# The gate product of the sixth attention unit on VectorE: one step moved between engines in a fused attention and two-layer expert kernel

## The chip, the core and the metric

The program runs on one core of one Trainium2 chip. The metric is the device time of one execution in microseconds (us); the time before is the median of three runs. The engines are named as in the profile: PE is TensorE's matmul stream and PEld its weight loads, DVE is VectorE, ACT is ScalarE, POOL is GpSimd, SP is SyncE, which issues the DMAs.

## What is computed

The reference is a gated linear attention (an mLSTM) over 2 batches, 8 heads, 768 positions and head size 40, followed by two dense layers over the 1536 tokens:

```
m_new = max(f + m, i);  C = exp(f+m-m_new)*C + exp(i-m_new)*outer(v, k)
n = exp(f+m-m_new)*n + exp(i-m_new)*k
y = sigmoid(o) * (C q) / max(|n.q|, 1)                    # per position
h = max(x@w1, x@w2, x@w3);  z = h @ w_out                 # 320 -> 768 -> 320
g = mish(z @ w_in);         out = g @ w_out2              # 320 -> 2048 -> 320
```

The change touches one product in the third line: the output gate sigmoid(o) times the reciprocal of the denominator.

## The kernel before, in words

The attention is cut into 12 units: 6 chunks of 128 positions by 2 batches, unit u being chunk u//2 of batch u%2. The sixth unit is u = 5. Within a unit everything has 128 positions on the partitions. `attend(u)` loads the unit, spreads the decay factors over a PSUM bank with 8 matmuls (`spread`, L141), scans them on DVE (`decay`, L126), forms the scores q.k on PE (`scores`, L164, 16 matmuls as the trace counts them) into the same two banks, multiplies the two on DVE (`decayed`, L169), scales values and keys on POOL (`values` L175, `keys` L186), and takes the sigmoid of the output gate on ACT into the tile `sg` (`gateo`, L190). `passed` (L152) and `queries` (L180) bring in the state of the chunk before.

`finish(u)` ends a unit. `numer` (L206, L208) forms numerator and denominator in one PSUM bank, tile `it`. `denom` takes the denominator: two small DVE steps (L214, L215), a reciprocal on DVE (L216), then the product sg = sg * den over 128 x 320 elements on the engine it is given (L218), GpSimd unless told otherwise. `gated` multiplies `it` by `sg` on DVE into the tile `xn` (L223) and lets ACT copy the last 64 columns once more as padding (L224). `transpose_x` turns `xn` into three 128 x 128 blocks on PE (L235): the first two blocks read what DVE wrote, the third one also reads what ACT copied. ACT then copies the result to `xh` (L237), and `lower_x` (L248, L249) forms the low part on ACT and POOL. `outer` (L258, 6 matmuls in the trace) and `carry` (L270, L272) update the state.

Beside the attention the first dense layer runs: `up(blk, m)` is three groups of eight matmuls (L345), each into a bank of its own; ACT copies the first bank out (L360), DVE takes the maximum with the other two (L362), ACT rounds (L364), POOL forms the low part (L365). In the stretch of the change these matmuls are what PE does between the attention's steps. The weights come as packed 64-bit numbers: ACT rescales both halves (`scaled`, L291 and L292), DVE merges them (`merge`, L299 and L301), and `split_lhs` splits the result into a high part on ACT (L312 to L314) and a low part on POOL (L315 to L317). The unpacked tile `dec` has two buffers, so L291 of a weight waits until POOL's L317 of the weight two before has read its buffer.

Units 0 to 3 are ordered by hand; there the fourth unit's product is already on VectorE. From unit 4 on, the order on each engine is made by a planner. The program is written as a list of steps,

```
PLAN0 = "w2 a4 w3 u0.1 a5 w4 b4 w5 w6 b5 a6 w7 w8 a7 u0.2 b6 u0.3 u0.4"
```

(`a` attend, `b` finish, `w` load a weight of the first layer, `u` up), followed by PLAN1 with three loads of the second weight (`o0 o1 o2`), more units and the `down` matmuls (L376 to L384). The planner goes through a timeline of its own estimated costs; whenever an engine is free there, it gets the earliest step of the list that is ready at that moment. Then the order is fixed, and on the chip each engine works through its own list in that order, each instruction waiting for its semaphores. Where an estimate and the chip differ, an instruction can wait at the head of its engine while others behind it could run. PE's order in the second dense layer (L659) is again written by hand.

Of the kernel before, what the change touches and what calls it, by code (L numbers as in the profile page):

```python
# [44 lines left out]
def mlstm_moe_kernel(ctx, tc, fi0, fir, qk2, q3, nat, w13, wo1, wi2, wo2, ident, bmask, out):  # L45
    nc = tc.nc
# [150 lines left out]
    def numer(u, ps=None):  # L197
        c, b = u // B, u % B
        t = unit[u]
        ps = itbank(f"it{u}") if ps is None else ps  # L200
        it = heads(ps[:, 0:H * VD], VD)
        vt = vps[u % 2]
        for g in range(3):
            h1 = min(3 * g + 3, H)
            if c > 0:
                nc.tensor.matmul(it[:, 3 * g:h1], t["cb"][:, g], st[b][:, 3 * g:h1], start=True, stop=False)  # L206
            for h in range(3 * g, h1):
                nc.tensor.matmul(it[:, h], t["dt"][:, h], vt[:, h], start=(c == 0), stop=(c == 0 or h == h1 - 1))  # L208
        t["it"] = it

    def denom(u, eng=nc.gpsimd):
        num = unit[u]["it"]
        den = a2.tile([P, H, 1], F32, tag="den", name=f"den{u}")
        nc.vector.tensor_scalar(den, num[:, :, D:VD], -1.0, 1.0, op0=ALU.mult, op1=ALU.max)  # L214
        nc.vector.tensor_tensor(den, den, num[:, :, D:VD], op=ALU.max)  # L215
        nc.vector.reciprocal(den, den)  # L216
        sg = unit[u]["sg"]
        eng.tensor_tensor(sg, sg, den.to_broadcast([P, H, D]), op=ALU.mult)  # L218

    def gated(u):  # L220
        t = unit[u]
        xn = a2.tile([P, 3 * P], F32, tag="xn", name=f"xn{u}")
        nc.vector.tensor_tensor(heads(xn[:, 0:DM], D), t["it"][:, :, 0:D], t["sg"], op=ALU.mult)  # L223
        nc.scalar.activation(xn[:, DM:3 * P], xn[:, 2 * P:DM], AF.Copy)  # L224
        t["xn"] = xn

    def transpose_x(u, xp=None, fill=0):
        xh, xl = xs[u // 4]
        col = u % 4 * L
        xn = unit[u]["xn"]  # L230
        xp = bank("sm", f"xp{u}") if xp is None else xp
        dummy(xp, fill)
        xp = xp[:, 0:3 * L].rearrange("p (j t) -> p j t", j=3)
        for j in range(3):
            unit[u]["pe"] = nc.tensor.transpose(xp[:, j], xn[:, j * P:(j + 1) * P], idt[:, 0:P])  # L235
        unit[u]["xp"] = xp
        return nc.scalar.activation(xh[:, :, col:col + L], xp, AF.Copy)  # L237

    def lower_x(u):
        xh, xl = xs[u // 4]  # L240
        col = u % 4 * L
        if u < B:
            xr = m1.tile([P, 3, L], F32, tag=f"hl{4 + u}", bufs=1, name=f"xr{u}")
            nc.scalar.activation(xr, unit[u]["xp"], AF.Copy)
            return lambda: nc.gpsimd.tensor_tensor(xl[:, :, col:col + L], xr, xh[:, :, col:col + L].bitcast(F32), op=ALU.subtract)
        if u >= 4:
            xr = a2.tile([P, 3, L], F32, tag="xr", bufs=1, name=f"xr{u}")
            nc.scalar.activation(xr, unit[u]["xp"], AF.Copy)  # L248
            return nc.gpsimd.tensor_tensor(xl[:, :, col:col + L], xr, xh[:, :, col:col + L].bitcast(F32), op=ALU.subtract)  # L249
        return nc.vector.tensor_tensor(xl[:, :, col:col + L], unit[u]["xp"], xh[:, :, col:col + L].bitcast(F32), op=ALU.subtract)  # L250

    def outer(u, sp=None, fill=0):
        sp = bank("sm", f"sp{u}") if sp is None else sp
        dummy(sp, fill)
        sp = sp[0:120, 0:9 * VD].rearrange("p (h e) -> p h e", h=9)
        kt, vt = kps[u % 2], vps[u % 2]
        for g in range(3):
            pe = nc.tensor.matmul(sp[:, 3 * g:3 * g + 3], kt[:, 3 * g:3 * g + 3].rearrange("p h e -> p (h e)"), vt[:, 3 * g:3 * g + 3], start=True, stop=True)  # L258
        unit[u]["sp"] = sp
        return pe  # L260

    def carry(u):
        c, b = u // B, u % B
        sp = unit[u]["sp"]
        if c == 0:
            return nc.vector.tensor_tensor(st[b], sp[:, 0:H], bmt[:, 0:H].unsqueeze(2).to_broadcast([120, H, VD]), op=ALU.mult)
        dc = unit[u]["dc"]
        for g in range(3):
            h1 = min(3 * g + 3, H)
            nc.scalar.activation(st[b][:, 3 * g:h1], st[b][:, 3 * g:h1], AF.Copy, scale=dc[:, g])  # L270
        for j in range(3):
            nc.vector.scalar_tensor_tensor(st[b][:, j::3], sp[:, j:H:3], bmt[:, j:j + 1], st[b][:, j::3], op0=ALU.mult, op1=ALU.add)  # L272
# [296 lines left out]

    def finish(u):  # L570
        numer(u)
        denom(u)
        gated(u)
        transpose_x(u)
        lower_x(u)
        if u < NU - B:
            outer(u)
            carry(u)

    act = dict(u=up, d=down, w=load_w13, o=load_wo, a=attend, b=finish)  # L580

    def follow(plan):
# [279 lines left out]
```

## Time and profile before

| what | us |
|---|---|
| median of three runs | 396.18 (396.0 to 398.92) |
| the profiled execution, whole | 398.92 |
| its span, first to last instruction | 397.1 |
| PE busy | 384.9 (97% of the span) |
| DVE busy | 192.3 (48%) |
| ACT busy | 186.9 (47%) |
| POOL busy | 150.0 (38%) |

The profile shows the profiled execution, so what is read from it is a difference within 397.1 us. Busy shares are averages over three stages: attention with the first layer's upper half, the rest of the first layer, and the second layer, where only PE is busy nearly all the time. The mean granted clock of TensorE over the span is 0.987 of full speed.

### The profile page before, as it was taken

What the parts mean: (1) busy time and instruction counts of PE and PEld (TensorE: products, weight loads), DVE (VectorE), ACT (ScalarE), POOL (GpSimd) and SP (SyncE); (2) the same over time, 40 slices, a digit from 0 to 9 for tenths busy, and PEclk for the clock granted to TensorE, in tenths of its full rate; (3) what the DMA queues carried; (4) which work ended last, traced back from release to release, by engine and by line L of the source; (5) the groups of instructions that cost most, each with busy time, mean ns of one, the idle gap of its engine ahead of it and who ended that gap; (6) DMA issues with size and microseconds to landing.
All of it is one profiled execution on the core that took longest, in us unless ns stands there. A gap on an engine that the chain in (4) does not pass through costs nothing.

```text
span 397.1 us, 7598 instructions
## 1 busy us (share of the span) xinstructions
PE 384.9 (97%) x3098; PEld 335.2 (84%) x3098; DVE 192.3 (48%) x297; ACT 186.9 (47%) x382; POOL 150.0 (38%) x151
## 2 busy tenths in 40 slices
PE   8999899899999999999999999998999999999996
PEld 4788788688988888888788789887989899999986
DVE  6899988579454294208621165657222131311212
ACT  3548877726433233165721386886242242423222
POOL 6666897845623133357831036565000020000000
PEclk9899999969999999999999999999999999999999
DMA  7697573634430030003500034500010000100001
GB/s 195 206 281 245 185 247 114 207 120 158 143 104 1 2 132 2 0 2 81 179 5 0 0 134 143 193 2 0 15 55 2 2 2 2 66 2 2 2 2 66
DMA packets 10415, 32.70 MB, mean 82 GB/s; under 512 B 1405, under 2 KB 4285, under 8 KB 10381
## 3 DMA queue, kind: packets, MB, share of 16 engines
q1 hardware_dynamic: 10381, 32.23, 25.0%
q8 instruction: 24, 0.39, 0.4%
q14 instruction: 10, 0.08, 0.1%
HBM read 30.26 MB, written 1.97 MB: 81 GB/s over the span
## 4 chain that ended last, share of the span: by engine, by line
PE 65%; DVE 11%; ACT 11%; POOL 5%; issue 4%; DMA 3%; POOLq 0%; DVEq 0%; ACTq 0%; SPq 0%
PE o L659 16%; PE h L659 15%; PE mm L345 15%; PE it L208 4%; DMA raw_w<-in_w_dram 2%; PE sc L164 2%; PE mz L376 2%; PE mz L377 2%; PE mz L378 2%; ACT g L687 2%; DVE dec_wo L299 2%; DVE dt L126 1%; ACT gh L686 1%; PE fp L141 1%; PE it L206 1%
## 5 line engine op out<-in xcount | busy, mean ns | idle before, releaser
L659 PE MATMUL h<-zh,wi 64*128 64x512 f32 x480 | 88.9, 392 | 2.4 <-ACT g L687 2.2
L659 PE MATMUL o<-wo,gh 64*128 64x320 f32 (+1 forms) x736 | 90.0, 306 | 0.0
L659 PEld LDWEIGHTS o<-wo,gh 64*128 64x128 f32 (+1 forms) x736 | 85.5, 185 | 1.5 <-issue 0.4
L688 DVE TENSOR_TENSOR gl<-g,gh 128x512 fp32r<-128x512 f32 x48 | 37.4, 785 | 98.7 <-ACT g L687 98.5
L659 PE MATMUL o<-wo,gl 64*128 64x320 f32 (+1 forms) x368 | 84.6, 306 | 0.0
L659 PEld LDWEIGHTS h<-zh,wi 64*128 64x128 f32 x480 | 66.9, 185 | 12.7 <-ACT g L687 4.5
L345 PE MATMUL mm<-xh,w 128*128 128x512 f32 x270 | 73.7, 400 | 1.9 <-DVE st L272 1.2
L659 PE MATMUL h<-zl,wi 64*128 64x512 f32 x240 | 70.2, 390 | 0.0
L659 PEld LDWEIGHTS o<-wo,gl 64*128 64x128 f32 (+1 forms) x368 | 68.0, 185 | 0.0
L686 ACT ACTIVATE gh<-h 128x512 fp32r<-128x512 f32 x48 | 28.9, 602 | 75.9 <-PE h L659 75.9
L345 PEld LDWEIGHTS mm<-xh,w 128*128 128x128 f32 x270 | 50.3, 191 | 12.9 <-ACT dc L156 1.3
L345 PE MATMUL mm<-xl,w 128*128 128x512 f32 x162 | 46.9, 397 | 0.2 <-DVE xl L250 0.2
L659 PEld LDWEIGHTS h<-zl,wi 64*128 64x128 f32 x240 | 43.6, 184 | 4.0
L365 POOL TENSOR_TENSOR hl<-zraw,hh 128x512 fp32r<-128x512 f32 x18 | 26.2, 1458 | 41.7 <-ACT hh L364 41.5
L362 DVE TENSOR_TENSOR zraw<-zraw,mm 128x512 f32<-128x512 f32 x36 | 24.5, 681 | 27.2 <-PE mm L345 24.4
L345 PEld LDWEIGHTS mm<-xl,w 128*128 128x128 f32 x162 | 30.4, 190 | 6.9 <-DVE xl L250 0.6
L619 POOL TENSOR_TENSOR zl<-zraw,zh 128x512 fp32r<-128x512 f32 x9 | 12.5, 1400 | 47.4 <-ACT zh L618 47.3
L687 ACT ACTIVATE g<-h 128x512 f32<-128x512 f32 x48 | 29.1, 606 | 0.0
L126 DVE TENSOR_TENSOR_SCAN dt<-fp,idr 128x512 f32<-128x512 f32 x24 | 28.1, 1206 | 0.0
L605 POOL TENSOR_TENSOR wo<-dec_wo,wo 128x640 fp32r<-128x640 f32 x8 | 14.8, 1850 | 33.7 <-ACT wo L604 33.0
L208 PEld LDWEIGHTS it<-vp,dt 128*128 128x128 f32 x192 | 25.0, 196 | 1.4 <-POOL vp L175 0.8
L208 PE MATMUL it<-vp,dt 128*128 128x41 f32 x192 | 25.5, 275 | 0.4 <-POOL vp L175 0.4
(137 smaller groups left out, 572.7 us busy)
## 6 DMA issues: line engine op xcount, KB each, us to landing
raw_wo<-in_wo_dram SPq DMA_DIRECT2D x11, 640.0 KB
na<-in_nat_dram SPq DMA_DIRECT2D x12, 484.0 KB
raw_w<-in_w_dram SPq DMA_DIRECT2D x9, 640.0 KB
raw_wi<-in_wi_dram SPq DMA_DIRECT2D x8, 640.0 KB
qall<-in_qk_dram SPq DMA_DIRECT2D x24, 160.0 KB
out_dram<-ob SPq DMA_DIRECT2D x12, 160.0 KB
q<-in_q_dram SPq DMA_DIRECT2D x10, 180.0 KB
idt<-in_ident_dram SPq DMA_DIRECT2D x1, 80.5 KB
```

What stands on the lines that cost most here:

```text
L126: nc.vector.tensor_tensor_scan(dtf[:, j * 512:(j + 1) * 512], unit[u]["fp"][j], idr, 0.0, op0=ALU.mult, op1=ALU.add)
L164: nc.tensor.matmul(scs[h % 2][:, (h // 2) * L:(h // 2 + 1) * L], qk[r:r + 64, 1, h // 2], qk[r:r + 64, 0, h // 2], start=True, stop=True)
L208: nc.tensor.matmul(it[:, h], t["dt"][:, h], vt[:, h], start=(c == 0), stop=(c == 0 or h == h1 - 1))
L345: nc.tensor.matmul(ps, a, r, start=(k == 0), stop=(k == 7))
L362: tops[blk, m] = nc.vector.tensor_tensor(top, top, pss[i], op=ALU.max)
L365: nc.gpsimd.tensor_tensor(ls, top, h.bitcast(F32), op=ALU.subtract)
L605: nc.gpsimd.tensor_tensor(w[:, 1], z, w[:, 0].bitcast(F32), op=ALU.subtract)
L619: nc.gpsimd.tensor_tensor(zl[:, j], zv[:, j], zh[:, j].bitcast(F32), op=ALU.subtract)
L659: mm = nc.tensor.matmul(out_, a, r, start=first, stop=last).ins
L686: mark[blk, m] = nc.scalar.activation(gh, ps, AF.Mish)
L687: nc.scalar.activation(g, ps, AF.Mish)
L688: low[blk, m] = nc.vector.tensor_tensor(gl, g, gh.bitcast(F32), op=ALU.subtract)
```

## The change

In `finish`, the unit with u = 5 hands VectorE to `denom`; all others hand GpSimd as before.

```
     def finish(u):
         numer(u)
-        denom(u)
+        denom(u, nc.vector if u == 5 else nc.gpsimd)
         gated(u)
         transpose_x(u)
         lower_x(u)
```

One instruction (L218, 128 x 320, float32) goes from POOL's list to DVE's. The planner lays out everything from there on anew.

## Rows read from the trace of the kernel before

**Rows 1.** The page, PE's granted clock in 40 slices of the span, tenths
```profile
PEclk9899999969999999999999999999999999999999
```

**Rows 2.** Four stretches: length, busy time of each engine (instructions), PEclk, DMA share, GB/s
```profile
41.00:43.00 2.00, 0.85 (x12) 0.69 (x8) 1.97 (x6) 2.00 (x7) 1.85 (x3) 1.00 0.00 0
...
76.78:78.73 1.95, 0.00 (x0) 0.03 (x1) 0.63 (x2) 1.40 (x3) 1.24 (x3) 1.00 0.17 58
...
80.66:87.07 6.41, 6.23 (x26) 5.18 (x26) 3.95 (x10) 1.21 (x5) 1.78 (x3) 0.50 0.46 148
...
88.00:194.00 106.00, 106.00 (x620) 91.07 (x620) 55.88 (x94) 46.28 (x96) 47.74 (x47) 1.00 0.19 64
```

**Rows 3.** The chain that ended last, around 77 us: start, us, engine, tile, line
```profile
77.34 0.73 POOL sg L218
```

**Rows 4.** PE's timeline, 73 to 81 us: start, us, line, tiles, [idle before <-releaser]
```profile
73.67 1.00 PE L141 MATMUL fp<-fzr,sel 128*128 128x128 f32 x8
74.52 1.35 PE L345 MATMUL mm<-xh,w 128*128 128x512 f32 x5
...
76.39 0.39 PE L345 MATMUL mm<-xh,w 128*128 128x512 f32 x1
78.73 0.53 PE L235 MATMUL xp<-idt,xn 128*128 128x128 f32 x3 [1.96 <-ACT hh L364]
...
79.66 0.51 PE L152 MATMUL cp<-fzr,sel 128*120 128x128 f32 x3
...
80.89 2.07 PE L164 MATMUL sc<-qall 64*128 64x128 f32 x14 [0.18 <-DVE dt L126]
```

**Rows 5.** DVE's timeline, 71 to 79 us
```profile
71.27 0.20 DVE L216 RECIPROCAL den<-den 128x8 f32<-128x8 f32 x1
...
72.55 1.47 DVE L362 TENSOR_TENSOR zraw<-zraw,mm 128x512 f32<-128x512 f32 x2
78.10 0.49 DVE L223 TENSOR_TENSOR xn<-it,sg 128x320 f32<-128x320 f32 x1 [4.07 <-POOL sg L218]
```

**Rows 6.** POOL's timeline, 71 to 80 us
```profile
71.48 1.30 POOL L315 TENSOR_TENSOR w<-dec_w,w 128x512 fp32r<-128x512 f32 x1
...
76.81 0.45 POOL L317 TENSOR_TENSOR w<-dec_w,w 64x128 fp32r<-64x128 f32 x1
...
78.67 1.29 POOL L365 TENSOR_TENSOR hl<-zraw,hh 128x512 fp32r<-128x512 f32 x1 [0.61 <-ACT hh L364]
```

**Rows 7.** ACT's timeline, 77 to 79 us
```profile
77.30 0.78 ACT L291 ACTIVATE dec_wo<-raw_wo 128x640 f32<-128x640 f32 x1 [1.84 <-POOL w L317]
77.97 0.62 ACT L364 ACTIVATE hh<-zraw 128x512 fp32r<-128x512 f32 x1
78.62 0.26 ACT L224 ACTIVATE xn<-xn 128x64 f32<-128x64 f32 x1
```

**Rows 8.** VectorE's only L218, in the hand-ordered part (unit 3)
```profile
32.81 0.49 DVE L218 TENSOR_TENSOR sg<-sg,den 128x320 f32<-128x320 f32 x1
```

**Rows 9.** A DVE and a POOL step side by side, 58 to 62 us
```profile
59.30 1.79 DVE L301 SCALAR_TENSOR_TENSOR dec_w<-raw_w,dec_w 128x640 int32<-128x640 int32 x1
...
58.90 1.51 POOL L315 TENSOR_TENSOR w<-dec_w,w 128x512 fp32r<-128x512 f32 x1 [0.33 <-ACT w L312]
```

**Rows 10.** The third transpose of unit 4 and what it waits for, 64 us
```profile
64.26 0.26 ACT L224 ACTIVATE xn<-xn 128x64 f32<-128x64 f32 x1
...
64.57 0.33 PE L235 MATMUL xp<-idt,xn 128*128 128x128 f32 x1
```

**Rows 11.** Unit 6 on ACT and PE, 96 to 100 us
```profile
97.77 0.80 ACT L292 ACTIVATE raw_wi<-raw_wi 128x640 int32<-128x640 uint32 x1 [1.50 <-DMA raw_wi<-in_wi_dram]
...
99.09 0.24 ACT L224 ACTIVATE xn<-xn 128x64 f32<-128x64 f32 x1
...
96.91 0.50 PE L376 MATMUL mz<-hh,wo 128*128 128x512 f32 x1
...
99.09 0.38 PE L235 MATMUL xp<-idt,xn 128*128 128x128 f32 x2
```

More of the change, by code (lines that the diff above doesn't have):

```diff
@@ L571, in finish @@
         numer(u)
-        denom(u)
+        denom(u, nc.vector if u == 5 else nc.gpsimd)
         gated(u)
```

## The prediction, made before the changed kernel was run

> **What bounds the kernel now.** I read the clock line of the page first, then busy times by stretch, the chain of waits, and last the timeline of each engine around the changed step. PE is the bound: between 88 and 194 us it is busy 106.00 of 106.00 us [rows 2], so whatever is won or lost at 87 us should arrive at the end, as long as the order behind stays good. The clock line has one low slice after the start, the ninth [rows 1]. By stretches that is 80.66 to 87.07 us, 6.41 us at a granted 0.50, the 1.2 GHz level [rows 2]. Just before it, from 76.78 to 78.73 us, PE does nothing for 1.95 us [rows 2]. A shorter gap, 1.15 us of the stretch from 41 to 43 us (2.00 less 0.85 busy), left the clock at 1.00 [rows 2] and its slice at 9 [rows 1].
>
> The gap belongs to unit 5. Its reciprocal is ready at 71.47 us (71.27 + 0.20) [rows 5], but the product waits on POOL until 77.34 us, behind L315 to L317 of weights 7 and 8 and one L249, and stands on the chain that ended last [rows 3, 6]. DVE idles 4.07 us for it, multiplies at 78.10 us [rows 5], and PE goes on with the transposes at 78.73 us [rows 4]. So the stretch loses 1.95 us of stall, 6.41 / 2 = 3.2 us of half clock, and about 0.2 us of PE (0.18 us before the scores at 80.89 [rows 4]) while the next scan, late behind the same product, empties the bank: 5.3 us. That is the largest sum the change can reach here.
>
> **What goes away.** POOL loses 0.73 us at 77.34 us [rows 3]. Worth nothing by itself: its next step, L365, waits for ACT until 78.67 us anyway [rows 6].
>
> **What is added.** DVE gets L218. The one such row took 0.49 us [rows 8]; no POOL step stood beside it. In unit 5 POOL starts L315 at 71.48 us [rows 6], the moment the product would start. The nearest row for that is L301, two SBUF operands beside an L315: POOL ended at 60.41 us, and DVE, which had started at 59.30, ended only at 61.09 us, 0.68 after [rows 9]. So the product costs between 0.49 us and 0.49 + 1.30 = 1.79 us; or POOL waits, and its list up to weight 8 slips by 0.49 us. I take 0.49 us on DVE and nothing on POOL, since the planner had two more DVE steps (L169) to put between. The Trainium skill, "SBUF — State Buffer", section "Who interferes with whom", says that a DVE instruction with two SBUF inputs and a GpSimd one that reads SBUF take turns, whichever started first holding the port to its end. By that rule one of the two ends would be met rather than a value between; rows 9 agree with it.
>
> Either way it is hidden. Product and multiply (0.49 each) go in front of or between the L169 and L362 steps, and `xn` is written by about 75 us at worst (71.47 + 1.79 + 0.49 + the 1.25 us of the two L169). Queued behind them on DVE are the two L362 [rows 5], which free the banks for PE's groups at 74.52 and 76.39 us [rows 4]. They move by 1.0 us (2.3 us at worst), to an end near 75.0 us; even that falls into the wait described next. No DMA is issued by the step.
>
> **What is late next.** The third transpose needs not only DVE's `xn` but ACT's padding copy L224. In unit 4 one sees it alone: L224 at 64.26 us, the third transpose at 64.57, 0.31 after [rows 10]. In unit 5, L224 ran at 78.62 us, behind L364 at 77.97, behind L291 of a later weight, which stood idle 1.84 us until POOL's L317 of weight 8 ended at 77.26 us [rows 6, 7]. The change leaves that L317 where it is. So the question is whether the planner puts L224 in front of that L291. I think not. `b5` stands before `w7` and `w8` in the list and yet POOL got the product only behind both, so on the planner's clock the reciprocal was not done when L317 of weight 8 was handed out. L291 is ready as soon as that one instruction (0.45 us [rows 6]) is over, while L224 is at least two DVE steps (0.49 + 0.49 us) behind the reciprocal. ACT gets L291 first, and on the chip L224 waits behind it: earliest 77.97 us, in L364's place, so the third transpose at 78.28 us.
>
> What changes then is what stands in front of that transpose on PE. With `xn` known earlier, the planner draws the transposes and `outer` forward, past the up matmuls that now fill 74.52 to 76.78 us. PE's idle time is 78.28 less its arrival there:
> - order as before: two transposes after 76.78 us (0.22 us), arrival 77.00, stall 1.28 us; against 1.95 + 0.2 before, 0.85 us won.
> - pulled forward behind the spread (0.85 us from 73.67 to 74.52) and two up matmuls (0.47): the two transposes and six `outer` matmuls cost 0.82 (0.93 us from 78.73 to 79.66 less one transpose [rows 4]), arrival 75.81, stall 2.47 us; 0.3 us lost.
> - pulled in front of the spread as well, after one up matmul (0.23): arrival 74.72, stall 3.56 us; 1.4 us lost.
>
> Two of these gaps are longer than the 1.95 us after which the clock fell, so I leave the 3.2 us of half clock in. If L224 stays behind L364 it comes 0.65 us later, and POOL's slip could add 0.49 us. The middle case is nearest to the planner's habit of filling a wait with up matmuls: +0.3 us. The term runs from -0.85 to +1.4 + 0.65 + 0.49 = +2.6 us. The profiled execution took 398.92 us (397.1 and 1.82 around it), so it would become 399.2; it stands 2.74 us above the median. I apply the difference to the median: 396.18 + 0.3 = **396.5 us**, with 395.3 to 398.8 as this case's own range.
>
> **Rivals.**
> 1. *ACT is not in the way.* L224 is planned before that L291. ACT is idle for the 1.84 us in front of it [rows 7], so the copy would run at once, the transposes would find `xn` complete, and stall, half clock and scan wait all go: 396.18 - 5.3 = 390.9 us. For it: the chain names the product and not L291 [rows 3]. Against it: the order argument above, which needs only that POOL's list was made by readiness. A smaller form keeps PE's order as before and has the clock survive a stall of 1.28 us, near the 1.15 us that it survived [rows 2]: 0.85 + 3.2 = 4.05 us, 392.1 us. Chances 0.22 and 0.06.
> 2. *The same stall opens at unit 6.* There L224 ran at 99.09 us, behind an L292 that waited 1.50 us for a DMA; PE did not notice, since nine `down` matmuls stood in front of the transposes, from 96.91 us on [rows 11]. The new order is made from a timeline that believes unit 5 is done earlier; if it also draws unit 6's transposes in front of those nine, PE reaches the third one at about 96.98 + 0.82 = 97.8 us and waits until 99.09 + 0.31 = 99.4: 1.6 us. This decides only if the clock falls, between 1.15 us (it did not) and 1.95 us (it did): 1.6 + 3.2 = 4.8 us on top of 396.5, 401.3 us. For it: behind 88 us there is no idle PE to lose without price [rows 2]. Against: the units behind 88 us depend on loads and up matmuls that the change does not touch. Chance 0.22, which takes in the like in a later unit.
>
> **How the numbers follow.** The forecast (no change that counts) has 0.50, rival 1 in both forms 0.28, rival 2 0.22. About 1% is what a measurement of this kernel can tell from no change, here 4.0 us; the forecast lies inside it with its whole range, both forms of rival 1 outside below, rival 2 outside above. So faster 0.28, same 0.50, slower 0.22. The range reaches from just below 390.9 to just above 401.3 us, to hold 8 in 10: 390.2 to 401.5.
>
> **What would show it.** Right: in the new trace DVE's idle time before `xn` of unit 5 is gone and `xn` is written before 76 us; L224 of unit 5 still starts near 78 us behind L291; PE still has one gap of 1.3 to 3.6 us before the third transpose, with up matmuls behind it that stood in front before; the ninth slice of the clock line is still low. Wrong by rival 1: L224 follows `xn` within 0.5 us and PE has no gap over 1 us between 70 and 90 us, with a clock of 1.00 there. Wrong by rival 2: a new idle stretch of PE behind 88 us, the clock low after it. Wrong altogether: if the order of the engines behind 100 us differs so far that no unit can be laid beside its former self.

## The result, and where the time came from

The changed kernel takes 401.61 us (median of four runs, 399.64 to 404.35) beside 396.22 us of the kernel before on the same chip: a ratio of 1.0122, 95% interval 1.0078 to 1.0167. The change costs about 4.8 us; 396.5 us had been forecast, with a range that ended at 401.5. By the ratio the earlier median of 396.18 us becomes 401.0 us, just inside that range; the median of the four runs is just outside. The clock does not explain the loss: two of the four runs had a mean clock of 1.000 and still took 399.64 and 400.31 us. All readings of this section come from the profiled execution, 404.35 us with a span of 402.6 us; the one of before was 398.92 us, so the two profiles are 5.43 us apart.

From the page of the changed kernel, the span, the busy times and PE's granted clock in 40 slices:

```profile
span 402.6 us, 7597 instructions
...
PE 388.7 (97%) x3098; PEld 336.2 (84%) x3098; DVE 195.3 (49%) x298; ACT 187.2 (46%) x382; POOL 148.1 (37%) x150
...
PEclk9899999889999999999999999999999999999999
```

PE has the same 3098 instructions and the same 97%, and is busy 3.8 us longer (384.9 before). The low clock falls in the eighth and ninth slices, where [rows 1] had it in the ninth. So neither share nor clock line shows where the time went. The start of the second dense layer narrows it down. The first L659 on PE's timeline of before:

```profile
221.05 0.73 PE L659 MATMUL h<-zh,wi 64*128 64x512 f32 x4
```

and of the changed kernel:

```profile
226.46 0.73 PE L659 MATMUL h<-zh,wi 64*128 64x512 f32 x4
```

The whole difference, 5.41 us, is there by then. Three stretches ahead of it, with the columns of [rows 2], before:

```profile
60.00:88.00 28.00, 25.72 (x150) 21.67 (x150) 20.23 (x34) 16.16 (x37) 18.75 (x22) 0.88 0.47 148
88.00:180.00 92.00, 92.00 (x558) 79.49 (x558) 44.49 (x82) 37.67 (x82) 37.19 (x38) 1.00 0.17 60
180.00:210.00 30.00, 29.28 (x129) 23.92 (x129) 16.90 (x19) 14.61 (x24) 18.76 (x17) 1.00 0.28 88
```

and after:

```profile
60.00:88.00 28.00, 25.39 (x148) 21.21 (x147) 21.86 (x34) 16.56 (x39) 17.99 (x22) 0.88 0.45 142
88.00:180.00 92.00, 92.00 (x543) 78.53 (x542) 44.62 (x82) 33.87 (x72) 31.60 (x33) 1.00 0.19 62
180.00:210.00 30.00, 28.38 (x122) 22.32 (x121) 17.03 (x18) 17.21 (x32) 22.37 (x21) 1.00 0.27 88
```

Read the number of PE instructions, not the busy time. Up to 88 us the changed kernel is two instructions behind. From 88 to 180 us PE is busy every moment at full clock in both, and yet starts 543 in place of 558. From 180 to 210 us it starts 122 in place of 129 and is idle 0.9 us more. That makes 24 instructions; what is left over at 210 us are matmuls of the first layer, which follow each other at about 0.226 us (8 in 1.81 us): 5.4 us. The first two of the 24, 0.5 us, are not the work of the change. At 72 us, where the orders of PE are still the same, PE of the changed kernel was already 0.51 us late (72.37 after 71.86 us), since a weight's DMA had come later in that execution: L292 on ACT started at 63.44 after 62.88 us. That leaves 4.9 us, close to the 4.8 us by the ratio.

**Unit 5, where the change was made.** DVE and POOL of the changed kernel, 72 to 74 us:

```profile
71.96 0.20 DVE L216 RECIPROCAL den<-den 128x8 f32<-128x8 f32 x1
72.20 1.62 DVE L218 TENSOR_TENSOR sg<-sg,den 128x320 f32<-128x320 f32 x1
73.85 0.49 DVE L223 TENSOR_TENSOR xn<-it,sg 128x320 f32<-128x320 f32 x1
```

```profile
72.18 1.29 POOL L315 TENSOR_TENSOR w<-dec_w,w 128x512 fp32r<-128x512 f32 x1
```

The product starts 0.02 us behind L315, and ends 0.35 us after it: 1.62 us, in place of the 0.49 us of [rows 8]. ACT, 74 to 79 us:

```profile
74.68 0.81 ACT L291 ACTIVATE dec_wo<-raw_wo 128x640 f32<-128x640 f32 x1 [1.08 <-POOL w L317]
75.60 0.79 ACT L292 ACTIVATE raw_wo<-raw_wo 128x640 int32<-128x640 uint32 x1
76.29 0.24 ACT L224 ACTIVATE xn<-xn 128x64 f32<-128x64 f32 x1
...
78.06 0.78 ACT L291 ACTIVATE dec_wo<-raw_wo 128x640 f32<-128x640 f32 x1 [1.17 <-POOL w L317]
```

and PE beside it:

```profile
74.48 0.41 PE L235 MATMUL xp<-idt,xn 128*128 128x128 f32 x2 [0.59 <-DVE xn L223]
74.73 0.58 PE L258 MATMUL sp<-vp,kp 128*120 128x123 f32 x4
76.58 0.48 PE L235 MATMUL xp<-idt,xn 128*128 128x128 f32 x1 [1.27 <-ACT xn L224]
```

The planner put L224 in front of the L291 that waits for weight 8 (78.06 us), but behind the one that waits for weight 7 (74.68 us) and behind an L292. `xn` is written at 74.34 us and its padding at 76.53. PE, whose transposes were drawn forward, waits twice, 0.59 + 1.27 = 1.86 us, where it waited 1.95 + 0.18 before [rows 2, 4]. Here nothing is lost and little is won. The half clock that follows is there as before [rows 2], now from 76.6 us on and of the same length (before, the granted clock was 0.50 from 80.3 to 87.1 us); the stretch in the columns of [rows 2]:

```profile
76.60:83.40 6.80, 6.80 (x23) 5.96 (x24) 4.04 (x7) 3.21 (x8) 4.90 (x7) 0.50 0.23 72
```

**Units 8 to 11, which the change does not touch.** PE at unit 8 before (its 16 scores L164 in one piece, 95.81 to 96.91 us, 1.10 us):

```profile
95.81 1.17 PE L164 MATMUL sc<-qall 64*128 64x128 f32 x16
96.91 0.50 PE L376 MATMUL mz<-hh,wo 128*128 128x512 f32 x1
```

and after:

```profile
97.57 0.48 PE L164 MATMUL sc<-qall 64*128 64x128 f32 x2
97.98 0.55 PE L235 MATMUL xp<-idt,xn 128*128 128x128 f32 x3
98.37 0.80 PE L258 MATMUL sp<-vp,kp 128*120 128x123 f32 x6
99.10 1.49 PE L164 MATMUL sc<-qall 64*128 64x128 f32 x14
100.51 0.53 PE L152 MATMUL cp<-fzr,sel 128*120 128x128 f32 x3
```

The same 16 scores take from start to next start 0.41 + 1.41 = 1.82 us. Units 9, 10 and 11 read the same way: 1.50, 1.95 and 1.50 us, where each had 1.09. That is 6.8 in place of 4.4 us, and no view calls it idle. The reason lies in line 164: head h reads row half h mod 2, and in program order the halves alternate. Before, the starts come in pairs, 6 to 14 ns apart, a pair every 111 ns: one matmul on each half. In the new order two things happen to them. In units 8 and 10 matmuls of `sc1` come in a block behind those of `sc0`, and most starts stand alone, 111 ns apart. In units 9 and 11 the pairs mostly stay, but the run is cut in two by the transposes and `outer` (in unit 11 by `numer` too), and each change from scores to something else or back takes some 0.1 us more (0.2 us to the next start in place of 0.11): 0.4 us. The Trainium skill, "TensorEngine Tiling (Array Packing)", section "Key Properties", says that different tiles can run matmuls in parallel; these starts agree for the two row halves, and show that the order of issue decides whether it happens.

**Behind 180 us.** Before, PE's timeline has one wait there:

```profile
195.44 1.43 PE L345 MATMUL mm<-xh,w 128*128 128x512 f32 x5 [0.72 <-DVE zraw L362]
```

and after three:

```profile
184.40 1.45 PE L345 MATMUL mm<-xh,w 128*128 128x512 f32 x5 [0.46 <-ACT zraw L360]
...
201.45 1.43 PE L345 MATMUL mm<-xh,w 128*128 128x512 f32 x5 [0.25 <-DVE zraw L362]
...
204.48 1.43 PE L345 MATMUL mm<-xh,w 128*128 128x512 f32 x5 [0.91 <-ACT zraw L360]
```

From start to start these cost 0.62 + 0.41 + 1.07 = 2.1 us more than a matmul does, against 0.88 us before: 1.2 us.

### The profile page after: what moved, and what is told of

It reads as the page before. It is cut to its first block, busy times and chain, and to the rows that moved or that the text cites. A ratio compares the mean times of both kernels' runs of the same rounds, so it can differ in the third digit from the quotient of the medians.

```text
span 402.6 us, 7597 instructions
## 1 busy us (share of the span) xinstructions
PE 388.7 (97%) x3098; PEld 336.2 (84%) x3098; DVE 195.3 (49%) x298; ACT 187.2 (46%) x382; POOL 148.1 (37%) x150
## 4 chain that ended last, share of the span: by engine, by line
PE 66%; ACT 13%; DVE 9%; DMA 7%; POOL 3%; issue 2%; ACTq 0%; DVEq 0%; POOLq 0%; SPq 0%
PE o L659 16%; PE h L659 15%; PE mm L345 14%; DMA raw_w<-in_w_dram 5%; PE it L208 4%; PE sc L164 3%; PE mz L376 2%; PE mz L377 2%; PE mz L378 2%; DVE dec_wo L299 2%; PE fp L141 2%; ACT g L687 2%; ACT gh L686 1%; PE it L206 1%; ACT dec_wo L291 1%
## 5 line engine op out<-in xcount | busy, mean ns | idle before, releaser
L659 PE MATMUL h<-zh,wi 64*128 64x512 f32 x480 | 88.9, 392 | 2.4 <-ACT g L687 2.3
L659 PE MATMUL o<-wo,gh 64*128 64x320 f32 (+1 forms) x736 | 90.0, 306 | 0.0
L659 PEld LDWEIGHTS o<-wo,gh 64*128 64x128 f32 (+1 forms) x736 | 85.4, 185 | 1.5 <-issue 0.4
L659 PE MATMUL o<-wo,gl 64*128 64x320 f32 (+1 forms) x368 | 84.7, 306 | 0.0
L659 PEld LDWEIGHTS h<-zh,wi 64*128 64x128 f32 x480 | 66.9, 185 | 13.0 <-ACT g L687 4.6
L345 PE MATMUL mm<-xh,w 128*128 128x512 f32 x270 | 74.2, 402 | 2.5 <-ACT zraw L360 1.4
L659 PE MATMUL h<-zl,wi 64*128 64x512 f32 x240 | 70.3, 390 | 0.0
L659 PEld LDWEIGHTS o<-wo,gl 64*128 64x128 f32 (+1 forms) x368 | 68.0, 185 | 0.0
L345 PEld LDWEIGHTS mm<-xh,w 128*128 128x128 f32 x270 | 49.9, 191 | 14.2 <-ACT zraw L360 2.2
L345 PE MATMUL mm<-xl,w 128*128 128x512 f32 x162 | 47.3, 399 | 0.2 <-DVE xl L250 0.2
L659 PEld LDWEIGHTS h<-zl,wi 64*128 64x128 f32 x240 | 43.6, 184 | 4.1
L362 DVE TENSOR_TENSOR zraw<-zraw,mm 128x512 f32<-128x512 f32 x36 | 24.5, 680 | 29.9 <-PE mm L345 26.4
L345 PEld LDWEIGHTS mm<-xl,w 128*128 128x128 f32 x162 | 30.8, 192 | 7.0 <-DVE xl L250 0.6
```

What stands on the lines that cost most here:

```text
L345: nc.tensor.matmul(ps, a, r, start=(k == 0), stop=(k == 7))
L362: tops[blk, m] = nc.vector.tensor_tensor(top, top, pss[i], op=ALU.max)
L659: mm = nc.tensor.matmul(out_, a, r, start=first, stop=last).ins
```

## The experiments

All kernels but the eleventh have each engine's order written out: every instruction of an engine follows a given neighbour, without a semaphore between them. So an order can be kept while one step changes its engine, or changed while the step stays. Ratios are to the kernel before, on the same chip, with the 95% interval; its medians there were 397.1 to 398.1 us.

**1 and 2. The step without the order, the order without the step.** In `e1_step_alone` the lists are those of before, but for one instruction:

```
 DVE:  ... L362 L362
+DVE:  L218 (sg, unit 5)
 DVE:  L223 (xn, unit 5) ...
-POOL: L218 (sg, unit 5)
```

> The order of before is kept on every engine; only the product of unit 5 goes to DVE, directly in front of the multiply, behind the two L362. Theory A (the new order of the engines made the change slow, not the step): 395.4 to 396.7 us, since the third transpose still waits for ACT's L224 behind L291 and L364; L224 starts at 77.9 to 78.6 us and PE's gap is 1.5 to 1.95 us. Theory B (the product on DVE, beside POOL, costs by itself): 399 us or more. Theory C (the wait for POOL alone made the gap): no gap over 0.5 us near 77 us and 394.2 us or less.

Measured: 396.56 us, ratio 0.9978 (0.9949 to 1.0008). The product took 0.48 us. L224 started at 78.49 us behind L291 and L364, and PE's gap was 2.40 us, since PE came 0.6 us earlier and had the first two transposes ahead of it:

```profile
76.01 0.38 PE L235 MATMUL xp<-idt,xn 128*128 128x128 f32 x2
78.79 0.33 PE L235 MATMUL xp<-idt,xn 128*128 128x128 f32 x1 [2.40 <-ACT xn L224]
```

In `e2_order_alone` the lists are those of the changed kernel, and L218 stands on POOL in front of L315 of weight 7.

> The order of the changed kernel on every engine, but the product of unit 5 back on POOL, directly in front of L315 of weight 7. Theory A (the order is the cost): 400 to 402.5 us, as the changed kernel, since POOL's product (0.73 us) starts at 72.2 us and delays POOL's list by about as much as the shared port delayed DVE's. Theory B (the engine is the cost): 396 to 397 us.

Measured: 402.06 us, ratio 1.0121 (1.0074 to 1.0169), the ratio of the change itself. So the step moved between engines costs nothing that these intervals can show, and the order that the planner made for it costs all. Theory A held in both; the gap in the first was larger than said.

**3 and 6. The scores.** `e3_scores_rejoined` is the changed kernel with the scores put together again, here unit 10 (numbers are heads):

```
-PE: L164 0 2 4 | L235 L258 | L164 1 3 5 6 7 | L152
+PE: L235 L258 | L164 0 1 2 3 4 5 6 7 | L152
```

> The changed kernel with its own order, except that the eight score matmuls of each of units 7 to 11 stand together again, alternating between the two halves of the rows, at the place of the last of them. Theory A (part of the loss is the broken alternation): the scores of units 8 to 11 take 1.1 us each again (6.78 us fall to 4.4 us) and the time is 2.0 to 2.8 us below the changed kernel's, 398.2 to 399.6 us. Rival (the waits of 183 to 205 us take the gain back, or what was put between filled a wait): 401 us or more with the scores at 4.4 us.

Measured: 400.03 us, ratio 1.0045 (1.0010 to 1.0080), 0.77% below the change, some 3 us, and 2.0 us below the second experiment on the same chip; the expected band, 398.2 to 399.6 us, was missed by 0.4 us. The scores of units 9 to 11 took 1.09 us again, as here in unit 10:

```profile
123.41 1.16 PE L164 MATMUL sc<-qall 64*128 64x128 f32 x16
124.50 0.53 PE L152 MATMUL cp<-fzr,sel 128*120 128x128 f32 x3
```

Unit 8's took 1.57 us: its first three starts stood alone, up to 0.27 us apart. The waits behind 180 us were the same three, 0.63, 0.42 and 1.07 us, so they do not hang on the scores.

`e6_scores_broken` is the counter-test: the kernel before, with nothing but the order of heads changed in units 8 to 11.

```
-PE: L164 0 1 2 3 4 5 6 7
+PE: L164 0 2 4 6 1 3 5 7
```

> The kernel before, product on POOL, with only the eight score matmuls of each of units 8 to 11 set so that the four of one half of the rows come first and then the four of the other, nothing between them. Theory A: each of the four units' scores takes 1.5 to 1.9 us in place of 1.1, and the time is 1.8 to 3.2 us above before. Rival (the alternation doesn't matter; in the changed kernel the scores only look longer since other matmuls stand between): scores at 1.1 us and before's time within 0.7 us.

Measured: 399.44 us, ratio 1.0063 (1.0033 to 1.0093), 2.5 us. Unit 8 again:

```profile
94.28 1.71 PE L164 MATMUL sc<-qall 64*128 64x128 f32 x16
95.92 0.50 PE L376 MATMUL mz<-hh,wo 128*128 128x512 f32 x1
```

1.64 us in place of 1.10, with no other matmul between; four units make 2.2 us. So the lost alternation costs by itself, without anything put between; in the changed kernel units 8 and 10 paid this and the cut, units 9 and 11 mostly the cut.

**5. Unit 5 alone.** `e5_unit5_alone` has the new order around unit 5 and that of before everywhere else.

```
-PE: L345 x2 L141 (unit 7) L345 x9 L235 x3 L258 x3 L152
+PE: L235 x2 L258 x2 L235 L258 L152 L141 (unit 7) L345 x11
```

> The order of before from unit 6 on, with the product on DVE, and only around unit 5 the order of the changed kernel (product and multiply in front of the L169 and L362, transposes, outer and L152 pulled in front of the spread, L224 in front of the L291 that waits for weight 8). Theory A (the loss arose behind unit 5, where the scores were broken up): PE's two gaps at unit 5 sum to 1.8 to 2.5 us, as in the changed kernel, and the time is within 1 us of before's median on this chip. Rival (the stall moved at unit 5 is the cost): 3 us or more above before.

Measured: 396.75 us, ratio 0.9983 (0.9949 to 1.0017). The gaps were 0.98 and 1.82 us, more than expected, and the time is still that of before. The stall that moved is not the cost. (The moves on DVE and ACT around unit 5, which the expectation names, are part of the run and are not printed here.)

**4 and 12. What the step is worth, and what it needs.** `e4_copy_first` is the first experiment with the copy moved on ACT:

```
+ACT: L224 (xn, unit 5)
 ACT: L291 (dec_wo, waits for POOL's L317 of weight 8)
 ACT: L364
-ACT: L224 (xn, unit 5)
```

> The first experiment (order of before, product on DVE) and one step more: on ACT the padding copy L224 of unit 5 goes in front of the L291 that waits for POOL's L317 of weight 8. Theory A: L224 starts at 75.4 us, PE has no gap over 0.3 us between 73 and 80 us, and the time is 1.9 to 2.2 us below the first experiment's, 393.6 to 394.6 us. Rival (PE only waits elsewhere, or the clock falls all the same): within 0.7 us of the first experiment's.

Measured: 394.69 us, ratio 0.9940 (0.9922 to 0.9958), faster than before and 1.9 us below the first experiment by the medians (1.5 us by the ratios), at the edge of the expected band. PE has no gap at unit 5 any more:

```profile
77.72 0.39 PE L345 MATMUL mm<-xh,w 128*128 128x512 f32 x1
77.95 0.49 PE L235 MATMUL xp<-idt,xn 128*128 128x128 f32 x3
78.28 0.80 PE L258 MATMUL sp<-vp,kp 128*120 128x123 f32 x6
```

Its profile shows a new one, though, at unit 6:

```profile
94.70 0.38 PE L235 MATMUL xp<-idt,xn 128*128 128x128 f32 x2
...
96.40 0.33 PE L235 MATMUL xp<-idt,xn 128*128 128x128 f32 x1 [0.90 <-ACT xn L224]
```

`e12_copy_first_pool` moves the copy and leaves the product on POOL.

> The kernel before, product on POOL, with only the copy L224 of unit 5 in front of the L291 that waits for weight 8: the fourth experiment without the change. Theory A (neither step gains alone, since the third transpose waits for both the product and the copy; only the two together open it): the product still ends at 78.1 us, L224 follows at 78.6 us, PE's gap stays 1.9 to 2.2 us and the time is within 1 us of before. Rival (the place of L224 on ACT is all that counts): the gap falls under 1 us and the time is 1.5 us or more below before.

Measured: 396.79 us, ratio 0.9993 (0.9967 to 1.0019). The gap stayed:

```profile
79.70 0.53 PE L235 MATMUL xp<-idt,xn 128*128 128x128 f32 x3 [2.03 <-DVE xn L223]
```

Product alone 0.9978, copy alone 0.9993, both 0.9940: two waits stand side by side in front of the third transpose, and only both together open it.

**7 and 8. The rest of the new order.** `e7_scores_and_tail` adds to the third experiment on ACT:

```
+ACT: L360 (the first behind 180 us)
 ACT: L386 L387
-ACT: L360
 ...
+ACT: L364 L360
 ACT: L312 L313 L314 (last wi) L735
-ACT: L364 L360
```

> The third experiment (scores of units 7 to 11 rejoined in the changed kernel) and two steps of ACT moved behind 180 us: one L360 in front of L386, and the L364 and L360 that PE waited for in front of the last L312. Theory A (these waits of the changed kernel are a cost of their own): PE's waits of 0.63 and 1.07 us behind 180 us go, 1.0 to 1.7 us below the third experiment. Rival (the chain of the weights is late in any case, the wait comes back further on): within 0.6 us of the third experiment, with a wait of about the same sum at a later L345.

Measured: 399.53 us, ratio 1.0026 (0.9990 to 1.0062), 0.19% or 0.75 us below the third by the ratios, which is less than the intervals are wide. The waits of 0.63 and 1.07 us went; one of 0.51 and one of 0.20 us came in their place at other L345, so 2.1 us of waits became 1.1 us. By the trace this is half of each theory: part of the waits came from the place of those steps, and part is there wherever they stand, since the weights' chain is late. The times cannot confirm either half.

`e8_all_mended` also puts L224 of unit 5 in front of the L291 that waits for weight 7.

> The experiment before this one, and on ACT the copy L224 of unit 5 in front of the first L291 of the wo weights, which waits for POOL's L317 of weight 7. Theory A: the third transpose follows within 0.5 us of the second, PE's gap before it (1.27 to 1.94 us) goes, and the time is 1.2 to 3 us below the experiment before, near the fourth experiment's (order of before with the copy first), 394 to 396.5 us. Rival (something else in the new order costs too): 397.5 us or more.

Measured: 396.31 us, ratio 0.9992 (0.9969 to 1.0014), 1.3 us below the seventh by the ratios and 3.2 us by the medians. The third transpose followed at 73.57 us with no wait. The time is inside the expected band, yet 0.5% above the fourth experiment. What is left is visible: 1.00 us before the first transpose, for `xn`, and scores that now come before DVE's scan is done:

```profile
92.68 0.49 PE L164 MATMUL sc<-qall 64*128 64x128 f32 x2
93.74 0.49 PE L164 MATMUL sc<-qall 64*128 64x128 f32 x4 [0.57 <-DVE dt L126]
```

**9 and 10. Further on from the best.** `e9_unit6_too` mends the gap that the fourth experiment opened at unit 6.

```
+ACT: L224 (xn, unit 6)
 ACT: L292 (raw_wi, waits for its DMA)
 ACT: L336
-ACT: L224 (xn, unit 6)
```

> The fourth experiment (order of before, product on DVE, copy of unit 5 first) showed a new gap of PE at unit 6: 0.90 us before the third transpose, since L224 stood behind an L292 that waited 1.46 us for a DMA. Here L224 of unit 6 goes in front of that L292. Theory A (the second rival of the prediction, the same stall one unit on, is what the fourth experiment gave back): the gap at 95 us goes and the time is 0.7 to 1.2 us below the fourth experiment's. Rival (PE, earlier again, meets a wait further on): within 0.4 us of it, with a new gap behind 96 us.

Measured: 394.39 us, ratio 0.9926 (0.9898 to 0.9954), the lowest of all. The gap at unit 6 is gone:

```profile
94.12 0.38 PE L235 MATMUL xp<-idt,xn 128*128 128x128 f32 x2
94.34 0.58 PE L258 MATMUL sp<-vp,kp 128*120 128x123 f32 x4
94.76 0.27 PE L235 MATMUL xp<-idt,xn 128*128 128x128 f32 x1
```

In the profiles the second layer starts 1.14 us earlier (216.58 after 217.72 us). About half of that, 0.58 us, was there before unit 6's transposes (the scores of unit 8 start at 90.84 after 91.42 us), so the mended gap is worth some 0.6 us in the trace. The medians are only 0.3 us apart and the intervals overlap: the trace shows the gap closed, the timed runs don't tell theory A from the rival.

`e10_tail_too` moves one L362 on DVE in front of the last L301.

> The experiment before this one, and on DVE the first of the two L362 that PE waited for at 191 us (0.88 us, in the kernel before at 194.3 us) in front of the L301 of the last wi weight. Theory A: that gap shrinks to under 0.3 us and the time is 0.5 to 0.9 us below the experiment before. Rival (the weights' chain, now later, makes PE wait behind it): within 0.3 us.

Measured: 395.46 us, ratio 0.9954 (0.9927 to 0.9981), slower than the ninth if anything. The expectation was wrong: with L301 later, L312 and the table load L735 on ACT are later, and the L360 behind them made PE wait longer than the wait that had been removed:

```profile
193.46 1.43 PE L345 MATMUL mm<-xh,w 128*128 128x512 f32 x5 [0.26 <-DVE zraw L362]
194.72 0.86 PE L345 MATMUL mm<-xl,w 128*128 128x512 f32 x3
196.48 1.43 PE L345 MATMUL mm<-xh,w 128*128 128x512 f32 x5 [0.91 <-ACT zraw L360]
```

**11. The planner told of the halves.** `e11_halves_in_turn` is the changed kernel, planned freely, with an edge without a semaphore from each head's matmul to the next in `scores`, from unit 4 on:

```
-            nc.tensor.matmul(scs[h % 2][:, (h // 2) * L:(h // 2 + 1) * L], ...)
+            mm = nc.tensor.matmul(scs[h % 2][:, (h // 2) * L:(h // 2 + 1) * L], ...)
+            if h and u >= 4:
+                tc.add_manual_dep(mm.ins, was, mybir.DependencyInfo(mybir.DependencyClass.NoSync, ...), ...)
+            was = mm.ins.name
```

> The changed kernel, planned anew with one rule more: from unit 4 on the eight score matmuls of a unit are issued in their alternating order (others may stand between them). Theory A (the planner, not knowing that two halves of the rows run side by side, paid for its order with the scores): the scores of units 7 to 11 sum to 5.4 to 6.2 us in place of 8.2, and the time is 1.5 to 3 us below the changed kernel's, 398.5 to 400 us. Rival (the new plan pays elsewhere): 401 us or more.

Measured: 400.89 us, ratio 1.0063 (1.0031 to 1.0095), 0.6% or 2.3 us below the change by the ratios, whose intervals overlap, and above the expected 398.5 to 400 us. The scores of units 7 to 11 sum to 7.2 us (1.37, 1.50, 1.70, 1.50, 1.09), 1.0 us less than in the changed kernel but more than expected: the order holds, but the planner still puts other matmuls into a pair. Unit 5's scores, whole in the changed kernel (1.10 us), are now cut as well (1.50 us). Behind 180 us one wait of 0.87 us is left, as in the kernel before, in place of 2.1 us. So the planner that keeps the order of heads probably loses less, but its new order differs in other places too, and the run does not say which of these differences gave the gain.

## Why the prediction was right or wrong

- *PE is the bound, and a gain at 87 us arrives at the end as long as the order behind stays good.* The condition was written down and then taken as met. It was not: behind 88 us PE, with no idle moment, started 15 instructions fewer up to 180 us, in the stretch that [rows 2] had shown as fully busy. This is the step that failed. The forecast costed unit 5 and rival 2 costed waits further on; a PE that is busy throughout and slower by its order stood in neither. It measured +2.4 us from the scores of units 8 to 11 and +1.2 us from the waits behind 180 us, 3.6 of the 5.4 us between the profiles; 0.5 us was there before the orders differ, and the other 1.3 us were not assigned one by one. Experiments 1 and 2 show that the order behind is the cause as a whole, 3 and 6 show the scores' part of it; the part of the waits is read from the trace, and experiment 7 is too close to the noise to confirm it.
- *The product is hidden, 0.49 to 1.79 us.* The length was right within its bounds and wrong in the value taken. Beside an L315 that had started just before, it took 1.62 us, near the upper bound that [rows 9] gave. The Trainium skill, "SBUF — State Buffer", section "Who interferes with whom", let one of the two ends be expected; 1.62 us agrees with the upper one, 0.14 us short of the estimate by that rule (1.27 us until L315 ends and 0.49 us after it). Nor was it hidden: PE, its transposes drawn forward, waited 0.59 us for `xn`. In the second experiment, with the same order and the product on POOL, that wait is gone and the one for the copy is 1.86 us, the same sum. As experiments 1, 2 and 5 show, this is not what made the kernel slower.
- *With the product early, the third transpose still waits for L224.* Right, and the core of the forecast: with the order kept, the step gave 0.2%, inside the measurement's uncertainty, and with the copy freed too 0.6%.
- *ACT gets that L291 first.* Wrong: in the new order L224 stands in front of it. But an earlier L291 and an L292 stand in front of L224, so the third transpose came at 76.58 us, not at 78.28 and not at once. A wait of the same kind was one weight nearer. Of the signs that were to show the forecast right, this one, L224 near 78 us, failed; `xn` was written before 76 us (74.34) as said.
- *PE's order.* The transposes were pulled in front of the spread, the dearest of the three cases (+1.4 us), but with the copy at 76.29 us the gaps sum to 1.86 us. Experiment 5 puts this whole part at no measurable cost.
- *The half clock is left in.* Right for the profiled execution: 76.6 to 83.4 us at a granted 0.50, the 1.2 GHz level, behind gaps of 0.59 and 1.27 us; before, as long (6.41 us of it in [rows 2]). Not for every run: two of the four had a mean clock of 1.000.
- *Rival 1, 390.9 us.* It overrated its own case. With both waits open the kernel gains 0.60% (interval 0.42 to 0.78%), 2.4 us, which is about the stall of 1.95 + 0.2 us alone. The 3.2 us of half clock stood in the profiled execution, 2.74 us above the median, and were taken off the median, which did not hold all of them: the other runs of before in that comparison were 396.0 to 396.25 us, and beside the experiments runs of before near 396 us had a mean clock of 0.996 (one 1.000), those near 399 us one of 0.986 to 0.991.
- *Rival 2, 401.3 us.* Its size came true by another mechanism. In the changed kernel unit 6 has no gap, and the granted clock stays at 1.00 behind the new waits at 184 to 205 us. It is luck that the measured time lies at the edge of the range and not far outside: this rival set the upper bound, and its mechanism did not occur. The forecast itself, 0.3 us of loss, missed 4.5 us. The mechanism itself exists: in the fourth experiment PE, earlier by what it had won, waited 0.90 us at unit 6 for L224 behind the L292 that waited for a DMA.

What stays open: why the planner's new timeline lets `sc1` fall behind `sc0` in units 8 to 11 when only unit 5 had changed was not traced through the planner. That `sc1` is late there because DVE frees its bank after that of `sc0` would be a reason, but no run tested it. And the experiments' parts don't add up to 4.8 us exactly: scores 3.0, waits 0.75, by ratios whose intervals are 1.4 to 1.8 us to each side.

## What to carry to other kernels

When a planner sets the order, a change of one step can change every order behind it; before costing the step, test it with the old order held, and the new order with the step taken back. A busy share of 100% does not say that an engine works at the same pace: count its instructions per stretch, and look for matmuls that had run side by side and no longer do. And where a transpose waits for two engines, look for what is queued in front of both; opening one wait alone gained nothing here.

## What the hardware showed that was not expected

Two matmuls of 64 rows on different row halves start 6 to 14 ns apart, and a pair starts every 111 ns; the same eight heads, one half after the other, took 1.64 us in place of 1.10. The chip did not put them in pairs again by itself: only three pairs formed, around the change of halves.

A gap of PE was not followed by the half clock each time. In the changed kernel 0.59 + 1.27 us were, over 6.8 us; in the second experiment, with the same order, a single gap of 1.86 us before the third transpose was not, as that transpose and the stretches 73 to 80 and 80 to 90 us of its profile show:

```profile
76.52 0.33 PE L235 MATMUL xp<-idt,xn 128*128 128x128 f32 x1 [1.86 <-ACT xn L224]
```

```profile
73.00:80.00 7.00, 5.14 (x34) 4.41 (x33) 4.34 (x8) 4.73 (x9) 5.13 (x8) 1.00 0.46 164
80.00:90.00 10.00, 10.00 (x69) 8.70 (x68) 8.92 (x15) 5.03 (x13) 7.30 (x8) 1.00 0.59 185
```

The kernel before differs in this from run to run: beside the first four experiments one run took 399.08 us at a mean clock of 0.987, another 395.3 us at 1.000. A fall seen in one profile is thus not part of the median until a second run shows it.
